# The first token tiles of a gated two-branch attention kernel: a third tile loaded ahead of two weight slices, and three partial groups over each slice

## Chip, cores and metric

The kernel runs on one core of a Trainium2 chip, in one launch. The metric is the device time of one execution in microseconds (us), here as the median over runs. The kernel before takes 482.97 us, the median of 4 runs that lie between 482.77 and 483.16.

## What is computed

Two attention blocks read the same x (2048 tokens, 1024 features, bfloat16), and a gate for each token mixes their outputs:

```python
g = _sigmoid((x * gate_w).sum(-1, keepdims=True))
a = _A_ref(x, A_wqkv, A_wo)     # linear attention
b = _B_ref(x, B_wqkv, B_wo)     # sliding window, 8 keys, two tokens apart
return g * a + (1 - g) * b
```

Both blocks begin with `x @ wqkv` (1024 by 3072, cut into q, k, v of 32 heads with 32 features) and end with `@ wo` (1024 by 1024). A uses phi(t) = (t + 1 where t > 0, else exp(t)) + 1e-6 on q and k, sums k^T v over all tokens, and divides by a normaliser. B takes a softmax over each token's 8 keys. Nearly all the arithmetic is in the eight 2048 x 1024 x 1024 products. The change lies in the first of them, B's values v = x @ wqkv_B[:, 2048:3072].

## The kernel before

**Layout.** The 2048 tokens form 16 tiles of 128, even tokens first, then odd ones (L1122). `xT` holds x transposed: 128 partitions, 8 feature chunks, 2048 tokens. A DMA transpose from HBM brings one tile of it (256 KB; `load_x`, L1315). Weights lie in four slots `ws[0]` to `ws[3]`, each 8 feature chunks by 1024 columns, used in halves of 512 columns. `load_w` (L1320) brings chunks d0 to d1 of one half; two chunks of a half are 256 KB.

**Order of the work.** The kernel is written as a list of operations (`P.op`), each with an engine, an assumed cost, what it reads and writes, and a priority (by default its place in the list). A planner (`Prog.schedule`, L122) plays this list through with the assumed costs: when an engine is free, it takes the ready operation with the lowest priority number. The order that it finds for each engine is fixed in the program, and `emit` (L208) puts semaphore waits where an operation depends on another engine or a DMA. So the queues of TensorE, SP and the others are strictly in the planned order on the chip. An operation marked "any" (the copies out of PSUM, `move`, L1372) is given to ScalarE or VectorE by the planner. It plans six times, with the bank use of the last plan as a guide, and keeps the plan with the shortest planned span (L1809 to L1815).

**The first stage** (L1325 to L1412) is B's v: for tiles 0 to 7 the first half of the columns, then the second half; then the same for tiles 8 to 15. One tile and half is eight matmuls (128x128 by 128x512) that add up over the eight chunks in one PSUM bank. `group` (L1340) sends the matmuls of chunks lo to hi as one operation, which waits as a whole for the data it reads. The result is copied to `vst` and stored to `vB_hbm` by SP (L1410). Seven banks are in the pool of this stage (L1338). Eleven matmuls on zeros run before it (L1382).

**The loads of the start** (L1325 to L1336), with their priorities: tile 0 (0) on SP; chunks 0-1 (0.1) and 2-3 (0.2) of the first weight half on the queue of ScalarE ("act"); tile 1 (0.25), chunks 4-5 (0.3) and 6-7 (0.4) on SP; tile t from 2 on (3 + t) on SP; then the second weight half (10.1 to 10.7). The stores of the first tiles have priority 10.9.

**The first two tiles** are interleaved (L1392 to L1402): two banks are taken at once. For the chunk ranges 0-3, 4-5, 6-7, tile 0 and then tile 1 are multiplied, in operations of two chunks. From tile 2 on, one operation does all eight chunks. A load of a later weight half is tied to the end of tile 2's group (`early`, L1386 and L1412: `after=[o]`, priority 21).

**Later stages**: q and k of B (from L1555) with the score blocks of the window, 18 in all (`fill` and `rest`, L1441 and L1469), threaded between the groups of matmuls; A's k and v (from L1612), with the sum over tokens; A's q, its normaliser and output (L1674 to L1734); B's output product and the mix (`final`, L1736). All these big products go through `group` or the loop at L1747.

Of the kernel before, what the change touches and what calls it, by code (L numbers as in the profile page):

```python
# [25 lines left out]
class Tile:  # L26
# [16 lines left out]
    def part(self, *idx):  # L43

        dims = list(self.shape[1:])
        strides = []
        s = self.size
        for n in reversed(dims):
            strides.insert(0, s)
            s *= n  # L50
        out = [self.lo]
        for d in range(len(dims) - 1):
            lo, hi = idx[d]
            out = [b + i * strides[d] for b in out for i in range(lo, hi)]
        lo, hi = idx[-1]
        return [(self.space, b + lo * self.size, b + hi * self.size, self) for b in out]
# [1060 lines left out]
def build_kernel(nc, A_x, A_wqkv, A_wo, B_x, B_wqkv, B_wo, gate_w, out):  # L1117
    del B_x
    S = A_x.shape[1]
    NT = S // 128  # L1120
# [52 lines left out]
    def hb(p0, p1, half):  # L1173
        return [("H%d" % half, p0, p1, None)]
# [64 lines left out]
    def plan(seen):  # L1239
# [75 lines left out]
        def load_x(t, prio):  # L1315
            e_, r = t // 8, t % 8
            return P.op("sp", lambda e: e.dma_start_transpose(xT[:, :, t * 128:(t + 1) * 128], x2[e_, r * 128:(r + 1) * 128, :]),
                        1.5, writes=[xT.part((0, 8), (t * 128, (t + 1) * 128))], prio=prio, chan="x%d" % t, lat=1.3)

        def load_w(slot, half, src, c0, prio, d0=0, d1=8, eng="sp", after=()):  # L1320
            n = d1 - d0
            return P.op(eng, lambda e: e.dma_start(ws[slot][:, d0:d1, half * 512:half * 512 + 512], src[:, d0:d1, c0:c0 + 512]), 0.4 + 0.2 * n,
                        writes=[ws[slot].part((d0, d1), (half * 512, half * 512 + 512))], prio=prio, chan="w%d_%d_%d" % (slot, half, d0), lat=0.55 * n, after=after)
# [2 lines left out]
        load_w(0, 0, Bw, 2048, 0.1, 0, 2, "act")  # L1326
        load_w(0, 0, Bw, 2048, 0.2, 2, 4, "act")
        load_x(1, 0.25)
        load_w(0, 0, Bw, 2048, 0.3, 4, 6)
        load_w(0, 0, Bw, 2048, 0.4, 6, 8)  # L1330
        for t in range(2, NT):
            load_x(t, 3 + t)
        for d in range(0, 8, 2):
            load_w(0, 1, Bw, 2560, 10.1 + 0.1 * d, d, d + 2)
# [3 lines left out]
        main = Pool(banks[0:7])  # L1338

        def group(bank, lhs, rhs, reads, lo=0, hi=8):  # L1340
            def fn(e):
                last = None
                for dc in range(lo, hi):
                    last = e.matmul(bank.ap(), lhs(dc), rhs(dc), start=(dc == 0), stop=(dc == 7))  # L1344
                return last
            return P.op("pe", fn, (hi - lo) * mm(512), reads=reads, writes=[bank.iv])
# [13 lines left out]
        def x_tile(t):  # L1360
            return (lambda dc: xT[:, dc, t * 128:(t + 1) * 128]), xT.part((0, 8), (t * 128, (t + 1) * 128))
# [4 lines left out]
        def w_half(slot, half):  # L1366
            return (lambda dc: ws[slot][:, dc, half * 512:half * 512 + 512]), ws[slot].part((0, 8), (half * 512, half * 512 + 512))
# [4 lines left out]
        def move(dst, src, n, bank, reg, scale=None, reads=()):  # L1372

            if scale is None:
                fd = lambda e: e.tensor_copy(dst, src())  # L1375
                fa = lambda e: e.activation(dst, src(), ACT.Copy)  # L1376
            else:
                fd = lambda e: e.tensor_scalar(dst, src(), scale, None, op0=ALU.mult)
                fa = lambda e: e.activation(dst, src(), ACT.Copy, scale=scale)  # L1379
            P.op("any", {"act": fa, "dve": fd}, {"act": act(n) + (0.1 if reads else 0.0), "dve": dps(n)}, reads=[bank.iv] + list(reads), writes=[reg])  # L1380
# [7 lines left out]
        for t, half in [(t, half) for b in ((0, 8), (8, NT)) for half in range(2) for t in range(*b)]:  # L1388
            xs, xr = x_tile(t)
            w, wr = w_half(0, half)  # L1390
            part = lambda d0, d1: ws[0].part((d0, d1), (half * 512, half * 512 + 512))
            if half == 0 and t == 0:  # L1392
                first = [main.next() for _ in range(2)]
                for d in (0, 4, 6):
                    n = 4 if d == 0 else 2
                    for i in range(2):
                        xi, xri = x_tile(i)
                        for c in range(d, d + n, 2):
                            o = group(first[i], xi, w, [xri, part(c, c + 2)], c, c + 2)
                bank = first[0]  # L1400
            elif half == 0 and t == 1:
                bank = first[1]  # L1402
            else:
                bank = main.next()
                step = 2 if t == 0 else 8
                for d in range(0, 8, step):
                    o = group(bank, xs, w, [xr, part(d, d + step)], d, d + step)
            vt, vs = vst.next()
            move(vt[:, :, 0:32], lambda bank=bank: bank.ap().rearrange("p (h d) -> p h d", d=32), 512, bank, vt.part((0, 16), (0, 32)))
            P.op("sp", lambda e, t=t, vt=vt, half=half: e.dma_start(vB_hbm[t * 128:(t + 1) * 128, half * 528:half * 528 + 528], vt[:, :, :].rearrange("p h d -> p (h d)")), 0.6, reads=[vt.all()],  # L1410
                 writes=[hb(t * 128, (t + 1) * 128, half)], chan="vst%d" % vs, lat=0.5, prio=10.9 if t < 8 and half == 0 else 5)
            if (t, half) in early:  # L1412
                load_w(*early[t, half], after=[o])
# [17 lines left out]
        main = Pool(banks[0:4])  # L1431
# [123 lines left out]
        for e_ in range(2):  # L1555
            if True:
                for j in range(8):
                    for isq in range(2):
                        for u in (2 * e_, 2 * e_ + 1):
                            bank = main.next()  # L1560
# [51 lines left out]
        for t in range(NT):  # L1612
            pkt, _ = pk.next()
            azt, _ = az.next()
            xs, xr = x_tile(t)
            for r in range(4):
                bank = main.next([SO[3]] if r == 2 else [])
# [26 lines left out]
        main = Pool(banks)  # L1644
# [166 lines left out]
    for _ in range(PASSES):  # L1811
        got = plan(seen)
        seen = got[2]
        if best is None or got[0].span < best[0].span:
            best = got  # L1815
# [56 lines left out]
```

## Time and profile before

The profile is of one execution. Its own time is 483.0 us.

| | us |
|---|---|
| median of the runs | 482.97 |
| the profiled execution's own time | 483.0 |
| its span, first to last instruction | 481.3 |
| TensorE matmuls busy | 476.6 |
| VectorE busy | 281.4 |
| ScalarE busy | 146.7 |
| GpSimd busy | 6.3 |
| one 128x128 by 128x512 matmul as recorded | 0.379 |
| one weight load (128x128) | 0.098 |
| eleven matmuls on zeros | 1.25 to 5.39 |
| first matmul of the first stage | 5.72 |

How to read it: times count from the span's start. PE is TensorE's matmuls, PEld its weight loads, which run beside them; DVE is VectorE, ACT ScalarE, POOL GpSimd, SP the engine that issues most DMAs. A small q (SPq, ACTq) marks the sequencer of an engine, which issues DMAs. "L1344" is a line of the kernel, and as `group` sends its matmuls from one line, the tiles that a line names (`ps_all<-w,xT`) say more than its number. Consecutive matmuls overlap in the record (0.379 us each, a new one every 0.216 us), so a full PE line is not in itself a sign of peak rate. Square brackets at a line's end give the idle time before it and what ended it. The granted TensorE clock was 1.0 in all 40 slices of the span.

### The profile page before, as it was taken

What the parts mean: (1) busy time and instruction counts of PE and PEld (TensorE: products, weight loads), DVE (VectorE), ACT (ScalarE), POOL (GpSimd) and SP (SyncE); (2) the same over time, 40 slices, a digit from 0 to 9 for tenths busy, and PEclk for the clock granted to TensorE, in tenths of its full rate; (3) what the DMA queues carried; (4) which work ended last, traced back from release to release, by engine and by line L of the source; (5) the groups of instructions that cost most, each with busy time, mean ns of one, the idle gap of its engine ahead of it and who ended that gap; (6) DMA issues with size and microseconds to landing.
All of it is one profiled execution on the core that took longest, in us unless ns stands there. A gap on an engine that the chain in (4) does not pass through costs nothing.

```text
span 481.3 us, 10218 instructions
## 1 busy us (share of the span) xinstructions
PE 476.6 (99%) x4403; PEld 224.1 (47%) x4403; DVE 281.4 (58%) x578; ACT 146.7 (30%) x234; POOL 6.3 (1%) x38
## 2 busy tenths in 40 slices
PE   8999999999999999999999999999999999999997
PEld 3444444444444544545454455444444444444443
DVE  3212337888687788556737565598588136743444
ACT  2111111135333345434434435255542130111000
POOL 4000000000000000000000000000000000000000
PEclk9999999999999999999999999999999999999999
DMA  9999991132014337423213446820184019910212
GB/s 210 250 215 322 352 368 42 55 105 82 1 35 140 87 108 142 98 66 77 75 35 86 99 129 162 231 45 2 18 243 135 0 19 251 217 17 2 89 68 89
DMA packets 72950, 57.37 MB, mean 119 GB/s; under 512 B 37953, under 2 KB 60865, under 8 KB 72898
## 3 DMA queue, kind: packets, MB, share of 16 engines
q1 hardware_dynamic: 72210, 56.07, 44.0%
q8 instruction: 35, 0.57, 0.5%
q10 hardware_dynamic: 688, 0.59, 0.4%
q14 instruction: 17, 0.14, 0.1%
HBM read 34.49 MB, written 13.76 MB: 100 GB/s over the span
## 4 chain that ended last, share of the span: by engine, by line
PE 98%; DMA 1%; DVE 0%; issue 0%
PE ps_all L1344 81%; PE ps_all L1747 11%; PE ps_all L1499 2%; PE ps_all L1464 2%; DMA xT<-in_A_x_dram 1%; PE ps_all L1588 1%; PE ps_all L1692 0%; PE ps_all L1664 0%; DVE o L1751 0%
## 5 line engine op out<-in xcount | busy, mean ns | idle before, releaser
L1344 PE MATMUL ps_all<-w,xT 128*128 128x512 bf16 x960 | 211.0, 379 | 0.3 <-DMA xT<-in_A_x_dram 0.3
L1344 PE MATMUL ps_all<-xT,w 128*128 128x512 bf16 x768 | 168.3, 379 | 0.0
L1344 PEld LDWEIGHTS ps_all<-w,xT 128*128 128x128 bf16 x960 | 92.2, 98 | 110.9 <-DMA xT<-in_A_x_dram 1.3
L1344 PEld LDWEIGHTS ps_all<-xT,w 128*128 128x128 bf16 x768 | 74.1, 98 | 89.4 <-issue 1.3
L1747 PE MATMUL ps_all<-w,qT 128*128 128x512 bf16 (+1 forms) x264 | 55.6, 373 | 0.0
L1747 PEld LDWEIGHTS ps_all<-w,qT 128*128 128x128 bf16 x264 | 25.9, 98 | 29.6
L1355 DVE TENSOR_SCALAR e<-e 128x512 bf16<-128x512 bf16 x64 | 18.5, 289 | 31.8 <-ACT e L1353 17.0
L1478 ACT ACTIVATE E<-ps_all 128x1824 bf16<-128x1824 f32 (+1 forms) x18 | 30.4, 1688 | 18.9 <-PE ps_all L1499 18.9
L1375 DVE CAST vst<-ps_all 128x512 bf16<-128x512 f32 x16 | 11.1, 694 | 41.7 <-PE ps_all L1344 41.7
L1751 DVE SCALAR_TENSOR_TENSOR o<-ps_all,gm,xT 128x512 bf16<-128x512 f32 (+1 forms) x25 | 18.0, 728 | 21.1 <-PE ps_all L1747 21.0
L1353 ACT ACTIVATE e<-ps_all 128x512 bf16<-128x512 f32 x32 | 19.1, 597 | 31.4 <-PE ps_all L1344 31.4
L1351 ACT ACTIVATE e<-ps_all 128x512 bf16<-128x512 f32 x32 | 19.1, 597 | 26.1 <-PE ps_all L1344 24.8
L1302 DVE TENSOR_TENSOR mx<-mx,kT 128x1024 bf16<-128x1024 bf16 x32 | 21.0, 686 | 9.1 <-ACT kT L1376 9.0
L1516 DVE TENSOR_TENSOR ot<-ps_all,rs 128x480 bf16<-128x480 f32 (+1 forms) x54 | 25.8, 506 | 0.0
L1302 DVE TENSOR_TENSOR mx<-mx,qT 128x1024 bf16<-128x1024 bf16 x32 | 21.0, 686 | 7.2 <-ACT qT L1379 7.0
L1376 ACT ACTIVATE az<-ps_all 128x512 bf16<-128x512 f32 x23 | 13.8, 600 | 36.3 <-PE ps_all L1344 36.3
L1376 ACT ACTIVATE vst<-ps_all 128x512 bf16<-128x512 f32 x16 | 9.6, 600 | 47.4 <-PE ps_all L1344 47.4
L1376 ACT ACTIVATE kT<-ps_all 128x512 bf16<-128x512 f32 x21 | 12.5, 597 | 36.8 <-PE ps_all L1344 36.8
L1379 ACT ACTIVATE qT<-ps_all 128x512 bf16<-128x512 f32 x19 | 11.3, 597 | 35.3 <-PE ps_all L1344 35.3
L1515 DVE RECIPROCAL rs<-ps_all 128x15 f32<-128x15 f32 (+1 forms) x54 | 9.4, 203 | 21.3 <-PE ps_all L1499 19.4
L1357 DVE SCALAR_TENSOR_TENSOR pk<-ps_all,e 128x512 bf16<-128x512 f32 x32 | 21.6, 679 | 0.1
L1379 ACT ACTIVATE xT<-ps_all,g 128x512 bf16<-128x512 f32 x10 | 6.9, 688 | 45.1 <-PE ps_all L1344 45.1
(73 smaller groups left out, 276.1 us busy)
## 6 DMA issues: line engine op xcount, KB each, us to landing
rb<-rc_hbm SPq DMA_DIRECT2D x32, 256.0 KB, 5.3
w<-in_A_wqkv_dram SPq DMA_DIRECT2D x6, 1024.0 KB, 9.0
v<-vB_hbm SPq DMA_DIRECT2D x36, 132.0 KB, 2.8
vB_hbm<-vst SPq DMA_DIRECT2D x32, 132.0 KB, 5.5
w<-in_B_wqkv_dram SPq DMA_DIRECT2D x4, 1024.0 KB, 8.6
xn<-in_A_x_dram SPq DMA_DIRECT2D x16, 256.0 KB, 2.6
out_dram<-o SPq DMA_DIRECT2D x15, 256.0 KB, 2.2
oB_hbm<-ot SPq DMA_DIRECT2D x36, 96.0 KB, 2.1
```

What stands on the lines that cost most here:

```text
L1302: P.op("dve", lambda e, m=m, op=op: e.tensor_tensor(m[:, 0:n], m[:, 0:n], src, op), 0.08 + n / 1920.0, reads=[m.all(), reg], writes=[m.all()],
L1344: last = e.matmul(bank.ap(), lhs(dc), rhs(dc), start=(dc == 0), stop=(dc == 7))
L1351: P.op("act", lambda e: e.activation(e_[:, :], bank.ap(), ACT.Exp), act(512), reads=[bank.iv], writes=[e_.all()])
L1353: P.op("act", lambda e: e.activation(e_[:, :], bank.ap(), ACT.Exp, accum_out=qe[:, col:col + 1]), act(512) + 0.1, reads=[bank.iv], writes= ...
L1355: P.op("dve", lambda e: e.tensor_scalar(e_[:, :], e_[:, :], 1.0, 1e-6, op0=ALU.min, op1=ALU.add), 0.25, reads=[e_.all()], writes=[e_.all()])
L1357: P.op("dve", lambda e: e.scalar_tensor_tensor(out=dst, in0=bank.ap(), scalar=0.0, in1=e_[:, :], op0=ALU.max, op1=ALU.add), dps(512), read ...
L1376: fa = lambda e: e.activation(dst, src(), ACT.Copy)
L1379: fa = lambda e: e.activation(dst, src(), ACT.Copy, scale=scale)
L1478: P.op("act", lambda e: e.activation(E[:, 0:32 * nq].rearrange("p (j q) -> p j q", j=4), ps[:, 4:8, 0:8 * nq], ACT.Exp), act(32 * nq), rea ...
L1516: P.op("dve", lambda e, r=r, src=src, dst=dst, m=m: e.tensor_tensor(dst, src()[:, :, 0:32], r[:, 0:m, None].to_broadcast([128, m, 32]), AL ...
L1747: last = e.matmul(bank.ap(0, f1 - f0), qT[:, dc, t * 128:(t + 1) * 128], ws[3][:, dc, f0:f1], start=(dc == 0), stop=(dc == 7))
L1751: P.op("dve", lambda e, bank=bank, o_=o_, t=t, n=n, i0=i0, i1=i1, tgt=tgt, c0=c0: e.scalar_tensor_tensor(out=o_[:, i0 * 128:i1 * 128].rear ...
```

## The change

One tile more is loaded ahead of the third and fourth slices (chunks 4-5 and 6-7) of the first weight half, and three tiles instead of two share each slice as partial groups:

```diff
         load_x(1, 0.25)
+        load_x(2, 0.27)
         load_w(0, 0, Bw, 2048, 0.3, 4, 6)
         load_w(0, 0, Bw, 2048, 0.4, 6, 8)
-        for t in range(2, NT):
+        for t in range(3, NT):
             load_x(t, 3 + t)
...
             if half == 0 and t == 0:
-                first = [main.next() for _ in range(2)]
+                first = [main.next() for _ in range(3)]
                 for d in (0, 4, 6):
                     n = 4 if d == 0 else 2
-                    for i in range(2):
+                    for i in range(3):
                         xi, xri = x_tile(i)
                         for c in range(d, d + n, 2):
                             o = group(first[i], xi, w, [xri, part(c, c + 2)], c, c + 2)
                 bank = first[0]
-            elif half == 0 and t == 1:
-                bank = first[1]
+            elif half == 0 and t < 3:
+                bank = first[t]
             else:
                 bank = main.next()
```

Tile 2's transpose moves from behind the two weight slices to ahead of them in SP's order. Tiles 0, 1 and 2 are each multiplied with chunks 0-3, then each with chunks 4-5, then each with chunks 6-7, in operations of two chunks. Tile 2 was one operation of eight chunks before. The list of operations is then planned anew, as in every build.

## The prediction

> **What bounds the kernel now.** I read the page first, then the chain that ended last in order of time, then the waits of TensorE's weight loads, then the first ten microseconds of the PE, PEld and SP timelines. The page gives the span and how full TensorE is:
>
> ```profile
> span 481.3 us, 10218 instructions
> PE 476.6 (99%) x4403; PEld 224.1 (47%) x4403; DVE 281.4 (58%) x578; ACT 146.7 (30%) x234; POOL 6.3 (1%) x38
> ```
>
> The chain of waits begins like this (start, length, what):
>
> ```profile
> 0.80 4.87 DMA xT<-in_A_x_dram
> 5.67 0.05 issue
> 5.72 122.77 PE ps_all L1344 x568
> ```
>
> So 5.72 us pass until token tile 0 has landed (issue 0.80 + 4.87 = 5.67). After that 568 matmuls fill 122.77 us, 0.216 us each, with nothing between them. Since the busy share of pipelined matmuls proves little, I checked starts: the 67 matmuls listed from 5.72 last 14.63 us, and (14.63 - 0.38) / 66 = 0.216. The stretch that the change rewrites is therefore already at the rate of the rest. Is something hidden there? The weight loads show it:
>
> ```profile
> 5.71 0.55 PEld L1344 LDWEIGHTS ps_all<-w,xT 128*128 128x128 bf16 x4 [0.81 <-DMA xT<-in_A_x_dram]
> 6.45 0.67 PEld L1344 LDWEIGHTS ps_all<-w,xT 128*128 128x128 bf16 x4 [0.19 <-DMA xT<-in_A_x_dram]
> 7.42 0.56 PEld L1344 LDWEIGHTS ps_all<-w,xT 128*128 128x128 bf16 x4 [0.30 <-DMA w<-in_B_wqkv_dram]
> 8.26 0.59 PEld L1344 LDWEIGHTS ps_all<-w,xT 128*128 128x128 bf16 x4 [0.27 <-DMA w<-in_B_wqkv_dram]
> 9.16 0.33 PEld L1344 LDWEIGHTS ps_all<-w,xT 128*128 128x128 bf16 x3 [0.31 <-DMA xT<-in_A_x_dram]
> ```
>
> Five times a weight load waits for a landing: tile 0, tile 1, weight chunks 4-5, chunks 6-7, tile 2. A load starts some 0.04 us after its landing (5.67 and 5.71). Yet the matmuls behind the last three start on the beat:
>
> ```profile
> 7.46 0.59 PE L1344 MATMUL ps_all<-w,xT 128*128 128x512 bf16 x2
> 8.32 0.59 PE L1344 MATMUL ps_all<-w,xT 128*128 128x512 bf16 x2
> 9.18 0.59 PE L1344 MATMUL ps_all<-w,xT 128*128 128x512 bf16 x2
> ```
>
> These are 0.04, 0.06 and 0.02 us after their loads. The waits are absorbed by the load's lead of one matmul, with almost nothing left over: four matmuls use 0.86 us and the transfers arrive 0.97, 0.84 and 0.90 us apart. The page can't show this; it takes the two timelines side by side. SP issues in this order:
>
> ```profile
> 0.80 2.80 SPq L1317 DMA_TRANSPOSE xT<-in_A_x_dram  x2
> 3.65 1.09 SPq L1322 DMA_DIRECT2D w<-in_B_wqkv_dram  x2
> 4.78 8.52 SPq L1317 DMA_TRANSPOSE xT<-in_A_x_dram  x6
> ```
>
> [...] 216 ns from 5.72 on, and 427 ns among the first warm-up matmuls. [...] loads of 0.10 us, matmuls 0.02 to 0.06 us after a load's start. [...] Here SP's first eight transfers do land in the order of issue.
>
> **The change, part by part.**
>
> (1) *Tile 2 ahead of the weight slices.* It takes SP 1.29 us to get past a tile (4.78 to 6.07). Tile 2 is issued at 3.65 instead of 4.78, chunks 4-5 at 4.94 instead of 3.65, chunks 6-7 at 5.58 instead of 4.29. Tile 3 stays at 6.07, and everything behind it too, because the same three DMAs are issued ahead of it. No byte is added.
>
> (2) *Three partial groups.* The same 24 matmuls and weight loads are sent in another order: tiles 0, 1, 2 over chunks 0-3 (matmuls 1-12), over 4-5 (13-18), over 6-7 (19-24). Tile 2's one instruction group becomes four, which adds a few waits but no matmul. With matmul 1 at 5.72 and 0.216 us each, due times (latest start of the weight load) are: tile 1 as before; tile 2 at matmul 9, 7.46; chunks 4-5 at matmul 13, 8.32; chunks 6-7 at matmul 19, 9.61; tile 3 at matmul 25, 10.91.
>
> When do they land? There is no trace of this order, so I bound it from both sides, each time as start of the weight load.
>
> Lower bound: the DMA engines are full (busy share 9 in nearly all slices here), so transfers keep the spacing that their kinds show. Tile 2 follows tile 1 by the 0.90 us that it now follows chunks 6-7: 6.45 + 0.90 = 7.35. Chunks 4-5: + 0.97 (6.45 to 7.42) = 8.32. Chunks 6-7: + 0.84 = 9.16. Against 7.46, 8.32 and 9.61 the stall is 0.00 us.
>
> Upper bound: each keeps its own time from issue to landing. These are the windowed answers for tile 2 and for chunks 4-5:
>
> ```profile
> xT<-in_A_x_dram SPq DMA_TRANSPOSE x1, 4.3
> w<-in_B_wqkv_dram SPq DMA_DIRECT2D x1, 256.0 KB, 3.7
> ```
>
> Tile 2: 3.65 + 4.3 + 0.04 = 7.99, 0.53 late. That moves the later due times to 8.85 and 10.14. Chunks 4-5: 4.94 + 3.7 + 0.04 = 8.68, no further stall; chunks 6-7 (3.9): 5.58 + 3.9 + 0.04 = 9.52, none. Tile 3 (4.0): 10.11 against 10.91, none. Sum: 0.53 us.
>
> I take 0.15 us, nearer the lower end: the time from issue to landing is mostly waiting behind other bytes on full engines, and there are fewer of those ahead of tile 2 now. A gain is excluded while TensorE runs on the beat from matmul 1: an earlier landing has no stall to remove. What the change does bring is slack for tile 3 and after, which was there (10.91 due, 10.11 landed).
>
> (3) *The end of the three groups.* Their last matmuls are 20, 22 and 24, so tile 0's copy out of its bank, at 8.95 in the timeline, moves to about 10.2, and all three (0.60 to 0.69 us each on two engines) are done by about 12. The first store of such a tile is issued at 15.58, behind the other weight half in SP's order: 3 us of cover, so nothing. Three banks of seven are held instead of two; the first group that needs a bank again is the eighth, at matmul 57 (17.8 us): nothing. The weight load tied to tile 2's last group is tied to the same matmul 24 and is issued at 36.20: nothing. If these covers were gone, the stores would push tiles 8 to 15 back, which are due from matmul 129 (33.4 us); tile 8 is issued at 18.08.
>
> (4) *The planner runs anew.* With its own costs tile 3's group starts 0.24 us earlier (13.29 for 13.53): I use this only for order, as evidence that the first 24 matmuls stay in the order of the text. On later engine choices and queue orders it can act like a small shove: normally zero, at the worst rival C.
>
> Sum on the profiled execution: 481.3 + 0.15, and 1.7 around it (its own time is 483.0), gives 483.1. The median of the runs shown, 482.97, lies 0.03 below that execution: the same.
>
> **The rivals.** A (forecast): stall of 0 to 0.53 us, 483.0 to 483.5.
>
> B, the change does what it seems meant for: in executions other than the profiled one tile 2 comes later and TensorE does wait for it before. Its load has 0.02 us left, so a jitter of 0.2 us would show whole, and the new order gives it back: 482.8. Against it: four runs within 0.39 us, and tile 2 merely swaps places with transfers that have as little slack.
>
> C, slower: the new plan upsets the order on DVE at the 18 score blocks further on. Already at 189.28 a weight load waits for DVE:
>
> ```profile
> PEld ps_all L1344 <- DVE ot L1516: 0.5, 2, 0.3
> ```
>
> Idle there is 0.27 us where 0.12 is usual, and the matmul follows 0.07 us later. A copy of 0.69 us (L1375) planned ahead of the multiply that frees the bank would stall TensorE by 0.69 - 0.07 = 0.62 us per block. Two blocks pass 0.97 us; four give 2.5 us, 485.5. For it: that order comes from a heuristic. Against it: only two such waits are in the trace, both hidden, and DVE is 58% busy.
>
> **How the numbers follow.** About 0.2%, 0.97 us, is what a measurement of this kernel can tell from no change. A 0.78; B 0.08; C 0.12; and 0.02 for a plan that happens to save over 0.97 us in changes of matmul form. A and B are within 0.2%: 0.86. A's own range is 482.8 to 483.6 with the spread of the runs. The range asked for takes in B and the mild end of C: 482.7 to 484.1.
>
> **What would show it.** Right: weight loads waiting at about 7.4 (tile 2), 8.3 (chunks 4-5), perhaps 9.2, one or two matmuls up to 0.5 us off the beat, the beat kept after that; tile 3 without a wait. Wrong: a hole over 0.6 us before matmul 13 (transposes in a row land slower than one by one), [...] TensorE idle behind DVE after 128 us, or a first matmul not at 5.7.

## The result, and the profile after

The changed kernel takes 483.74 us (median of 40 runs, 483.01 to 484.16); the kernel before takes 483.05 us (60 runs, 482.46 to 483.79). The ratio is 1.0013, with a 95% interval of 1.0008 to 1.0017: 0.6 to 0.7 us slower, inside the range given (482.7 to 484.1), and 0.14 us above what the forecast case alone was meant to cover (482.8 to 483.6).

The page after says as little as the page before:

```profile
span 482.0 us, 10217 instructions
PE 477.4 (99%) x4403; PEld 224.3 (47%) x4403; DVE 282.9 (59%) x581; ACT 145.0 (30%) x231; POOL 6.2 (1%) x38
```

TensorE is "99%" in both, although the span grew by 0.7 us. The timeline of its matmuls has the answer (start, length, count, idle time before and what ended it):

```profile
5.92 2.88 PE L1345 MATMUL ps_all<-w,xT 128*128 128x512 bf16 x12
9.21 2.98 PE L1345 MATMUL ps_all<-w,xT 128*128 128x512 bf16 x13 [0.41 <-DMA w<-in_B_wqkv_dram]
```

Twelve matmuls, then a break, then matmul 13, which waits for weights. Matmul 12 starts 0.38 us before the end of its piece, at 5.92 + 2.88 - 0.38 = 8.42. Without the wait matmul 13 would have started at 8.64, and it starts at 9.21: a hole of 0.58 us. (The 0.41 us in the brackets counts from the recorded end of matmul 12, and so leaves out the part in which matmuls overlap.) The chain that ended last now begins like this; before, it held tile 0's DMA and then nothing but matmuls:

```profile
0.80 1.38 SPq L1317
2.18 0.06 issue
2.24 1.38 SPq L1317
3.62 0.04 issue
3.66 1.57 SPq L1317
5.23 0.04 issue
5.28 3.89 DMA w<-in_B_wqkv_dram
9.17 0.05 issue
9.21 2.98 PE ps_all L1345 x13
```

Read upward from the bottom: matmul 13 waited for chunks 4-5, which were 3.89 us under way from their issue at 5.28; SP could not issue them earlier because it was busy issuing three tiles, the third for 1.57 us. The weight loads agree:

```profile
5.76 0.31 PEld L1345 LDWEIGHTS ps_all<-w,xT 128*128 128x128 bf16 x2 [0.54 <-issue]
6.26 2.04 PEld L1345 LDWEIGHTS ps_all<-w,xT 128*128 128x128 bf16 x10 [0.19 <-issue]
9.21 1.84 PEld L1345 LDWEIGHTS ps_all<-w,xT 128*128 128x128 bf16 x10 [0.91 <-DMA w<-in_B_wqkv_dram]
```

Of the five waits for a landing one is left: tile 2 is in time, chunks 4-5 are not. After the hole the two kernels take the same time. The last 184 matmuls start at 440.22 before and at 441.05 after. From matmul 13 to there it is 440.22 - 8.32 = 431.90 us before and 441.05 - 9.21 = 431.84 us after.

Matmul 13 itself comes 0.89 us later than before (9.21 for 8.32), more than the hole. The other 0.31 us arose earlier, at the start: in this execution the matmuls on zeros still ran at a beat of 0.427 us when tile 0 was there, so matmul 1 started at 5.92 instead of 5.72, and matmul 2 another 0.12 us late. That belongs to the execution, not to the change: in the second profile of the changed kernel matmul 1 starts as late, at 5.97, because tile 0 lands at 5.84 instead of 5.67, and no beat is lost behind it. As the weights alone decide when matmul 13 may go (9.21 and 9.15 in the two profiles), what the change costs is their time less the time at which the old order gets there: 8.32 in the profile of before, 8.51 in that of the fourth experiment below, which has the old order of loads. The differences, 0.64 to 0.89 us, lie around the 0.69 us between the medians.

### The profile page after: what moved, and what is told of

It is laid out like the page before. It is cut to its first block, busy times and chain, and to the rows that moved or that the text cites. A ratio compares the mean times of both kernels' runs of the same rounds, so it can differ in the third digit from the quotient of the medians.

```text
span 482.0 us, 10217 instructions
## 1 busy us (share of the span) xinstructions
PE 477.4 (99%) x4403; PEld 224.3 (47%) x4403; DVE 282.9 (59%) x581; ACT 145.0 (30%) x231; POOL 6.2 (1%) x38
## 4 chain that ended last, share of the span: by engine, by line
PE 97%; SPq 1%; DMA 1%; DVE 0%; issue 0%
PE ps_all L1345 80%; PE ps_all L1748 11%; PE ps_all L1465 2%; PE ps_all L1500 2%; PE ps_all L1589 1%; SPq L1317 1%; DMA w<-in_B_wqkv_dram 1%; PE ps_all L1693 0%; PE ps_all L1665 0%; DVE o L1752 0%
## 5 line engine op out<-in xcount | busy, mean ns | idle before, releaser
L1377 ACT ACTIVATE kT<-ps_all 128x512 bf16<-128x512 f32 x18 | 10.7, 597 | 37.6 <-PE ps_all L1345 37.6
```

## The experiments

Three theories. **I**: SP issues chunks 4-5 later, by the time that a third transpose in a row takes it, and they keep their time from issue to landing. **S**: the late landing was an accident of one execution. **P**: the new plan costs the time further on. From the fifth run on a rival to I is **Q**: 256 KB more ahead in the queue is what counts, whatever SP does. All runs are timed against the kernel before on the same chip: 483.03 us beside the first four, 483.06 us beside the last three.

**1. The changed kernel again.** No edit.

> The changed kernel as it is, for a second profile and a timing beside the kernel before. Theory I (chunks 4-5 are issued by SP 1.6 us later and keep their 3.7 to 3.9 us from issue to landing): the weight load of matmul 13 again waits until 9.1 to 9.3 us, a hole of 0.5 to 0.9 us, time +0.5 to +0.9 us over before. Theory S (the landing at 9.17 in the first profile was one late pair of DMA engines, 14 of 16 were done at 8.45): the load starts at 8.4 to 8.6, the hole is 0.1 to 0.3 us, and the slowdown of the runs is somewhere else. Theory P (the new plan's order on VectorE and ScalarE costs it): the hole doesn't matter, TensorE has holes after 128 us.

Measured: 483.56 us, ratio 1.0012 (1.0006 to 1.0019).

```profile
5.94 1.42 PEld L1345 LDWEIGHTS ps_all<-w,xT 128*128 128x128 bf16 x8 [0.72 <-issue]
7.52 0.70 PEld L1345 LDWEIGHTS ps_all<-w,xT 128*128 128x128 bf16 x4 [0.16 <-DMA xT<-in_A_x_dram]
9.15 1.84 PEld L1345 LDWEIGHTS ps_all<-w,xT 128*128 128x128 bf16 x10 [0.92 <-DMA w<-in_B_wqkv_dram]
```

The load for matmul 13 waits until 9.15 again, and the hole is 0.60 us. As an accident of one execution, S falls. But it had seen something that is there again. The trace has 16 completion counts for each of these transfers, and the landing is the last of them. For chunks 4-5 in the first profile, 14 were in by 8.45 and the last came at 9.17; here 11 were in by 8.41 and the other five came from 8.92 to 9.11. Matmul 13 was due at 8.64 and 8.56. So in both profiles it waits for the last few counts. Tile 2's wait (load at 7.52) is absorbed.

**2. The load order alone.** Two partial groups as before:

```diff
         load_x(1, 0.25)
+        load_x(2, 0.27)
...
-        for t in range(2, NT):
+        for t in range(3, NT):
```

> The load order of the change, but two partial groups as before: chunks 4-5 are now due at matmul 9 (7.46 us), not 13 (8.32). Theory I: landing at 9.1 to 9.2 as in the changed kernel, so a hole of about 1.7 us before matmul 9, time +1.5 to +1.8 us over before. Theory S: landing near 8.45, hole 1.0 us, time +0.8 to +1.1 us. Theory P: nothing near 1 us, as its plan differs from the changed kernel's.

Measured: 484.59 us, ratio 1.0032 (1.0020 to 1.0045), +1.56 us.

```profile
9.02 0.55 PEld L1345 LDWEIGHTS ps_all<-w,xT 128*128 128x128 bf16 x4 [1.73 <-DMA w<-in_B_wqkv_dram]
```

The weights come at the same time (load at 9.02) and are due four matmuls earlier. The hole, now ahead of matmul 9, is 1.40 us, 0.3 below I's forecast: matmul 1 started 0.17 us later than in the profile of before, and the weights came somewhat sooner than forecast. The third group is thus worth some 0.8 us by itself (1.40 against 0.60 us of hole; 1.03 us between the medians): it puts off the due time by 0.86.

**3. Tile 2 between the two slices.**

```diff
-        load_x(2, 0.27)
+        load_x(2, 0.35)
```

> Three partial groups, tile 2 issued between chunks 4-5 and chunks 6-7. Matmul order: tiles 0 and 1 over chunks 0-3 and 4-5, tile 2 over 0-5, then all three over 6-7. Due: chunks 4-5 7.46, tile 2 8.32, chunks 6-7 9.61. VectorE's and ScalarE's planned orders are the changed kernel's. Theory I: chunks 4-5 land at 7.4 as before, tile 2 at 8.3 to 8.6, chunks 6-7 at 9.2 to 9.5: hole of 0 to 0.3 us, time within +0.0 to +0.3 us of before, clearly under the changed kernel. Theory S: the same landings, +0.0 to +0.3 us. Theory P: as slow as the changed kernel, +0.5 to +0.9 us.

Measured: 483.30 us, ratio 1.0009 (1.0000 to 1.0017).

```profile
6.03 4.88 PEld L1345 LDWEIGHTS ps_all<-w,xT 128*128 128x128 bf16 x24 [0.81 <-issue]
```

24 weight loads in one piece: no hole at all. The orders on VectorE and ScalarE are those of the changed kernel in the trace too, and the hole is gone, so P has nothing left to explain. The excess of 0.27 us is at the edge of what the runs can tell. Its profile shows only a late start (matmul 1 at 6.06, tile 0 having landed late), which no edit here explains.

**4. The three groups alone.** Tile 2's load stays where it was:

```diff
-        load_x(2, 0.27)
...
-        for t in range(3, NT):
+        for t in range(2, NT):
```

> Three partial groups with the load order of before: the planner leaves every engine's order as in the kernel before, tile 2 is only cut into four operations. All theories: within 0.15 us of before; its profile is a second look at the landings of the old order (7.4, 8.2, 9.1 us).

Measured: 483.22 us, ratio 1.0005 (0.9996 to 1.0013).

```profile
5.93 6.42 PE L1344 MATMUL ps_all<-w,xT 128*128 128x512 bf16 x29 [0.56 <-DMA xT<-in_A_x_dram]
```

No hole, and no difference that can be told, as it should be when no engine's order changes. The median is 0.19 us above that of before, a little outside the 0.15 us expected, which shows how far medians of such series stray. The second to fourth experiments together put the cause in the order of the loads: that order alone costs 1.56 us, and three groups cost nothing that can be told while chunks 4-5 stay ahead of tile 2.

**5. Tile 2 without the transpose.** The same 256 KB by a plain DMA, so that tile 2's x enters the products untransposed:

```diff
-        load_x(2, 0.27)
+        P.op("sp", lambda e: e.dma_start(xT[:, :, 256:384], x2[0, 256:384, :].rearrange("p (c f) -> p c f", f=128)),
+             1.5, writes=[xT.part((0, 8), (256, 384))], prio=0.27, chan="x2", lat=1.3)
```

> The changed kernel, but tile 2 is loaded by a plain DMA of the same 256 KB, without the transpose (so tile 2's x enters the products untransposed). Theory I (chunks 4-5 are late because SP needs 1.6 to 1.8 us to get past a third transpose in a row, and they keep 3.6 to 3.9 us from issue to landing): SP passes tile 2 in 0.5 to 0.6 us, issues chunks 4-5 at 4.2 to 4.3, they land at 7.9 to 8.4, the hole before matmul 13 is under 0.2 us, time -0.4 to -0.7 us against the changed kernel. Theory Q (it is the place behind 256 KB more in the queue, whatever SP does): landing still near 9.1, hole 0.5 to 0.7 us, time as the changed kernel.

Measured: 483.20 us, ratio 1.0000 (0.9991 to 1.0009).

```profile
3.56 0.58 SPq L1329 DMA_DIRECT2D xT<-in_A_x_dram  x1
4.20 1.90 SPq L1322 DMA_DIRECT2D w<-in_B_wqkv_dram  x2
```

```profile
8.16 0.55 PEld L1346 LDWEIGHTS ps_all<-w,xT 128*128 128x128 bf16 x4 [0.56 <-DMA xT<-in_A_x_dram]
8.90 2.19 PEld L1346 LDWEIGHTS ps_all<-w,xT 128*128 128x128 bf16 x11 [0.19 <-DMA w<-in_B_wqkv_dram]
```

SP is past tile 2 in 0.58 us and issues chunks 4-5 at 4.20, their wait is absorbed, and the runs take the time of the kernel before, as I says. But I's landing was wrong: load at 8.90, not 7.9 to 8.4, nearer Q's 9.1. Tile 2, too, came later than as a transpose (load at 8.16 instead of 7.52), and the chain of this execution goes through it:

```profile
3.56 4.56 DMA xT<-in_A_x_dram
8.12 0.05 issue
8.17 3.84 PE ps_all L1346 x17
```

Matmul 9 starts at 8.17 instead of 7.94: a hole of 0.23 us that neither theory had. With it and a late start (matmul 1 at 6.22) chunks 4-5 are due only at 9.04, which helped to hide their wait. So this run does not decide between I and Q: the hole is smaller than the 0.58 and 0.60 us of the changed kernel, but this execution reaches its last matmul no earlier than the second profile of the changed kernel (478.53 and 478.56), so its profile does not account for the shorter time of the runs.

Neither theory gives the landing. Chunks 4-5 took 4.7 us from issue to landing here, and that time is no constant elsewhere either: for chunks 6-7 it was 3.30 us in the third experiment and 3.08 us in the seventh. Nor is SP's time for a transfer fixed by its kind: the slice right behind the cheap tile 2 took SP 1.38 us (4.20 to 5.58), for 0.59 us in the changed kernel.

**6. Two tiles ahead.** The suspected wait doubled:

```diff
         load_x(2, 0.27)
+        load_x(3, 0.28)
...
-        for t in range(3, NT):
+        for t in range(4, NT):
```

> The changed kernel with tile 3 too issued ahead of chunks 4-5, without a fourth partial group: the suspected wait doubled. Theory I: chunks 4-5 are issued at 6.7 to 7.2, land at 10.4 to 10.9, hole before matmul 13 of 1.9 to 2.4 us, time +1.9 to +2.4 us over before. Theory Q: one transfer more, 0.9 us: landing at 10.0, hole 1.5 us, time +1.4 to +1.6 us over before.

Measured: 485.12 us, ratio 1.0043 (1.0026 to 1.0060), +2.06 us.

```profile
0.80 6.07 SPq L1317 DMA_TRANSPOSE xT<-in_A_x_dram  x4
6.92 1.09 SPq L1322 DMA_DIRECT2D w<-in_B_wqkv_dram  x2
```

```profile
10.67 0.33 PEld L1346 LDWEIGHTS ps_all<-w,xT 128*128 128x128 bf16 x3 [1.76 <-DMA w<-in_B_wqkv_dram]
```

Issue at 6.92, 3.7 us to landing, load at 10.67: issue and landing are as I said (Q: 10.0). The hole before matmul 13 is 1.43 us, smaller than I's, because matmul 1 started at 6.12 and this execution had lost 0.5 us more before matmul 13: tile 2 cost 0.13, and matmuls 2 and 3 came at a beat of about 0.43 us. The time is in I's range.

**7. Chunks 4-5 on ScalarE's queue.**

```diff
-        load_w(0, 0, Bw, 2048, 0.3, 4, 6)
+        load_w(0, 0, Bw, 2048, 0.3, 4, 6, "act")
```

> The changed kernel with chunks 4-5 issued from ScalarE's queue behind chunks 2-3, so that no transpose stands ahead of them. Theory I, if the DMA engines have room: they land by 7.4, tile 2 stays near 7.5, no hole over 0.2 us, time near before (-0.5 to -0.7 against the changed kernel). Theory Q (bytes decide, the engines are full): tile 1 comes late (7.0 or later against due 6.6) and tile 2 at 8.3 or later against due 7.5: holes of 0.8 us in sum ahead of matmul 9, time +0.5 to +0.9 us over before, no better than the changed kernel.

Measured: 483.81 us, ratio 1.0016 (1.0009 to 1.0023).

```profile
7.67 3.35 PEld L1345 LDWEIGHTS ps_all<-w,xT 128*128 128x128 bf16 x17 [1.10 <-DMA xT<-in_A_x_dram]
```

No transpose stands ahead of the weights now, and the wait only moves to tile 1: load at 7.67 instead of 6.45, a hole of 0.77 us before matmul 5. Here Q is right: chunks 4-5 cost no wait any more, and tile 1 comes 1.22 us later.

**Issue or engines?** The DMA engines' busy share between 5.6 and 9.6 us (40 slices of 0.1 us, in tenths, with GB/s) says more; here the kernel before and the changed one:

```profile
DMA  9998999999999999999999969999999999999965
GB/s 292 294 352 307 317 297 236 307 379 379 379 358 328 379 348 379 348 272 310 300 289 292 108 133 292 289 289 289 267 282 287 287 238 256 289 289 292 239 149 131
```

```profile
DMA  9999999999996139779887999998876669789989
GB/s 287 289 252 276 289 292 297 289 289 289 287 211 51 51 133 236 276 266 297 297 287 277 328 389 328 369 402 292 282 208 174 179 151 159 184 215 172 184 141 113
```

From 6.9 to 7.1 us, 1.6 us after chunks 4-5 were issued, the engines of the changed kernel fall to 1 and 3 tenths: the packets of tile 2 are through and few of the weights are there yet. In those 0.2 us 18 packets move, none of them under 512 B; from 5.9 to 6.6 us, while tiles came in, all 790 were. The kernel before moves 73 from 6.9 to 7.1 us. The second profile of the changed kernel and the load order alone show the same dip (down to 2 tenths); the kernel before, tile 2 between the slices and the groups alone don't. So here the engines run dry because the weights are issued late. After the gap comes a slow patch, at 6 to 9 tenths, in which the last counts of chunks 4-5 come long after the others. The price of the change is the two together; how they share it is not shown.

## Why the prediction came out as it did

The forecast was right that a late landing would stall the first 24 matmuls, that nothing would be gained and that nothing would be lost later. But it had the wrong transfer. The only stall in its sums was tile 2's, 0.53 us at the upper bound; chunks 4-5 were at nothing in both bounds. It was the other way round: tile 2 cost nothing, chunks 4-5 cost 0.58 and 0.60 us, more than the upper bound and four times the 0.15 us taken. That the time lies inside the range is in part luck: 483.74 is in the part that the range has for the mild end of rival C, which did not happen.

*The upper bound.* It let tile 2's stall put off the due time of chunks 4-5 and so hid theirs. With tile 2 in time, the forecast's own terms make it 4.94 + 3.7 + 0.04 = 8.68 against 8.32, or 0.36 us. The profile adds 0.34 us for the later issue (5.28 for 4.94) and some 0.2 us for the time to landing (3.89 for 3.7), and takes off 0.3 us for the late start: together the 0.58 us, within the rounding.

*Tile 2 is issued earlier.* Right: 3.66 us (forecast 3.65). It landed so that its load could start by 7.5, near the lower bound (7.35), and not at the upper one (7.99), in both profiles of the changed kernel. No stall arose there.

*It takes SP 1.29 us to get past a tile.* This term failed. That was tile 2's own time behind two weight slices; as the third tile in a row it took 1.57 us, 1.79 us in the second profile, 1.88 us in the sixth experiment and 2.80 us in the seventh. Chunks 4-5 were issued at 5.28 and 5.44, not at 4.94. Tile 3 did not stay at 6.07 either (6.42 and 6.58), but its slack covered that. The warning was in the profile of before: one tile of its row took 1.81 us (6.07 to 7.88).

*Lower bound: the DMA engines are full.* This failed too, and it was why I leaned to the lower end. In the old order a transfer does mostly wait behind others on full engines: of tile 2's 4.3 us from issue to landing (4.78 to 9.12), 3.4 had passed when the slice ahead of it landed (8.22). In the new order the engines were at 1 to 6 tenths for 0.3 us. A weight slice takes SP 0.46 to 0.59 us in the profiles of before and after, and lands 0.84 to 0.97 us behind the transfer ahead of it in that of before; a tile takes SP 1.24 us or more, up to 1.81 us in the first 12 us of the old order, and lands 0.7 to 1.0 us behind the transfer ahead of it (tiles 1 to 3 before, 1 and 2 after). In the old order two slices after two tiles rebuilt SP's lead over the engines; three tiles in a row use it up. The three transfers behind tile 1 landed within 2.7 us of it before (6.41 to 9.12) and within 3.4 us after (6.38 to 9.82).

*Due times.* Right: tile 3 was in time, chunks 6-7 caused no second hole, and the third group moved the due time by the 0.86 us expected, which the second experiment confirms.

*Ends of the groups, stores, banks: nothing.* Right. The new plan puts six stores ahead of tile 8 instead of five; that tile is due after 33 us, and no matmul waited.

*The planner, rival C.* It did reorder VectorE, ScalarE and SP, but not the lines of TensorE's queue, and from matmul 13 to the last 184 the two kernels differ by 0.06 us. So nothing was saved in changes of matmul form either. They have a price: in the profile of before 0.32 us pass from the start of the last of 40 products (128x128 by 128x512) to that of the first score matmul (64x64 by 64x114; 137.37 to 137.69), 0.10 us more than the beat. *Rival B* fell: the runs got slower, not faster, and neither profile with the old order of loads (before and the fourth experiment) has a wait of a matmul for tile 2 that the new order could give back.

*The signs of being wrong.* Two of them came close or came true. The hole before matmul 13 was 0.58 and 0.60 us where over 0.6 was named, but not for the reason given: transposes in a row did not land slower one by one (tile 2 took 3.75 and 3.88 us from issue to landing, against 4.3 forecast), they were issued slower. And matmul 1 was not at 5.7 but at 5.92 and 5.97; it was at 5.93 in the fourth experiment too, so that sign told nothing about the change.

**Left open**: the slow patch after the gap. In the trace the 16 completion counts of chunks 4-5 spread over 1.0 to 1.2 us in all three profiles with the new order (8.0 to 9.2), and over 0.2 us or little more in the kernel before and in the fourth and fifth experiments. In the sixth it was tile 2's own counts that spread, over 0.9 us; in the seventh the engines fell to 3 tenths at 8.2 us, and the counts of chunks 6-7 behind that dip spread over 0.4 us only. So the patch does not simply follow from the gap, and without it matmul 13 would hardly have waited. Why some counts come late behind three tiles in a row is not shown.

Nothing here beats the kernel before, and a reason can be read off: in the three profiles where the first 24 matmuls run without a hole (before, third and fourth experiments), the last matmul starts 472.2 to 472.5 us after the first, and none of these edits was meant to start the first one sooner.

## What to carry to other kernels

Before moving a transfer forward in a queue, add up two clocks: how long the issuing engine needs for it, and how long the DMA engines do. A transfer that is dearer to issue than to carry (a tile here: 1.24 us or more on SP, 0.7 to 1.0 us from landing to landing while the DMA engines are full, at 9 tenths) spends the issuer's lead, and what stands behind it can then land later than its turn, as chunks 4-5 did here (9.17, with matmul 13 due at 8.64). Take the issue time from a place with the same neighbours, and don't carry a time from issue to landing over as a constant: for 256 KB it was 2.8 to 4.9 us in the first 12 us of the profiles of before and after. When one transfer's stall puts off the due time of the next, also add up the case in which the first one is in time. And judge a reordering by due times: look for waits that the lead of the weight loads absorbs (one matmul, 0.22 us here), because a schedule with matmuls on the beat has nothing to give back.

## What was not expected of the hardware

The beat of 0.427 us, about twice the 0.216 us of the products, ended at 4.6 us in the profile of before and near 6.2 us in that of the changed kernel, with the same eleven matmuls on zeros; in the sixth experiment it lasted to 6.9 us. What ends it is not shown. The granted clock of the page is 1.0 throughout in both, so only the starts of the matmuls show the slower beat. Of the change's cost it is no part, but it moves single profiles by some 0.3 us, as much as half of what was to be explained.

A plain DMA of a tile to the same place was no faster than the transpose: its 256 KB landed 1.3 us after tile 1 (6.84 and 8.12 in the fifth experiment), the transposed one 0.9 to 1.0 us after tile 1 in the two profiles of the changed kernel (6.55 and 7.48; 6.38 and 7.41). It was cheaper to issue, 0.58 us on SP, but part of that came back in the next issue: SP was past tile 2 and both slices at 6.10 there, at 6.38 and 6.53 in the two profiles of the changed kernel.
